# Three tiles of a chunked linear attention kernel: the transpose of r and k moved from TensorE to a DMA

## The chip, the cores and the metric

The kernel runs on one core of one Trainium2 chip. The metric is the device time of one execution in microseconds (us). Of a changed kernel, the time is told against runs of the kernel before on the same chip.

## What is computed

The reference has two parts. The first is a linear attention with a decaying state, for 4 batches and 8 heads of 768 steps and 48 features:

```
for t in range(S):
    cur = einsum('bhd,bhe->bhde', u * k[t], v[t])
    y[t] = einsum('bhd,bhde->bhe', r[t], state + cur)
    state = w[t][:, :, :, None] * state + einsum('bhd,bhe->bhde', k[t], v[t])
```

The second part takes y as 3072 rows x of 384 numbers. A gate picks the two largest of 8 logits x @ w_gate and weighs them by a softmax. The output is x plus the weighted sum of two adapters (x @ A[e]) @ B[e] of rank 16.

## The kernel before

**Tiles.** The 3072 rows are cut into 24 tiles of 128 steps, six for each batch. Within a batch a tile has index c = t % 6, and a state S passes from tile to tile; c = 0 starts afresh.

**Stages of one tile.** They are small functions, named in the plan:

- ln, csA, csB: the logarithm of w (ScalarE) and its running sum (TensorE, into the accumulator cs_ps).
- expP, expN: exp of the sum and of its negative (ScalarE, L251 and L255).
- mult (L271, the multiply at L276): r times the one and k times the other in one VectorE instruction. The result is one of four fixed buffers rk2, 128 steps x (2, 4, 2, 64) in bf16: for r and for k, four pairs of heads, each pair padded to 128 columns.
- tr (L320, L324): eight TensorE transposes of 128 x 128 blocks into the accumulator trp. trev (L328, through the helper's line L301): ScalarE copies it to the buffer rkT, of which there are three.
- amm (L333, L339): for each of the eight heads the product of transposed k and transposed r, into a_ps. aev (L343, L345): VectorE masks it into at.
- kv (L352): adds k times v into the state's accumulator. sev and szero copy it out and blank the blocks that aren't wanted.
- ymS (L373): the state's part of y, with the transposed r of rkT as weights. ymA (L383): the part within the tile.
- rkp, xk, xkev, dg, dgev, dv, ba: the term with u. xs takes y out of the accumulator.
- lg, g1, gexp, g2, g3, g4: logits and gate, for batches of one to four tiles. z, zw, zTm, zTev: adapters' inner part.
- d (L516): the outer product and, for some tiles, x itself, into an accumulator. oev (L523): the copy to one of six result buffers, by ScalarE (L295) or VectorE (L528). store (L531, L532): a DMA to the output, issued by the sync queue.

**Order.** Nothing reorders the work: the string PLAN names each step with its tile and, behind the dot, the engine that it takes. Every engine executes its own instructions in the order of the plan, and waits at each for what it needs. This holds for the sync queue too: a DMA whose data isn't there holds up those behind it. Around the change the plan runs, on that queue, load of w for tiles 22 and 23, store:7, store:8, store:4, store:9, store:6, store:10, store:13 and so on. On TensorE tr:18 stands ahead of amm:18, tr:19 behind amm:18 and ahead of amm:19, and tr:20 between amm:19 and amm:20; a mult stands ahead of its tr:

```
mult:18 ymS:17 tr:18 rkp:20 ... aev:17 ... trev:18 dg:18 d:9.2 xs:16 mult:19 amm:18 ... oev:9.2 ...
aev:18 csB:20 xk:16 tr:19 expN:20 d:8.2 kv:19 mult:20 ... trev:19 ... amm:19 sev:19 xkev:17 d:10
oev:8.2 dv:18 csB:21 kv:20 ymA:18 aev:19 oev:10 tr:20 ... trev:20 amm:20 ...
```

Above, "..." stands for steps of the plan that are left out.

Of the kernel before, what the change touches and what calls it, by code (L numbers as in the profile page):

```python
# [8 lines left out]
BF16 = mybir.dt.bfloat16  # L9
# [31 lines left out]
csB:9 g3:3 mult:8 tr:8 szero:6 xs:5 xk:5 g4:3 dgev:7 expN:9 csA:10 dv:6.1 ymA:6 ba:6.1 dv:7 zw:3 aev:7 sev:7 ymS:7  # L41
xkev:5 kv:8 expP:10 rkp:10 lg:4 zTm:3 ba:7 trev:8 rkp:9.1 xs:6.1 sev:8 ymA:7 csB:10 zTev:3.1 mult:9 xs:7 szero:8
amm:8 load_w:14 xk:6 tr:9 szero:7.1 aev:8 d:0.2 d:1 expN:10 xkev:6 trev:9 oev:0.2 rkp:11.1 mult:10 oev:1 load_v:16
kv:9 csA:11 dg:8 dg:9 amm:9 expP:11 aev:9 d:3 dgev:9 csB:11 d:2.2 xk:7 dv:8 tr:10 sev:9 oev:3 expN:11 szero:9 dv:9.1
ymS:8 xkev:7 csA:12 lg:7 store:3 trev:10 ymA:8 ba:8 dg:10 lg:5 amm:10 oev:2.2 kv:10 xs:8 mult:11 lg:6 expP:12 csB:12
ln:14 xk:8 rkp:15 expN:12 g1:7 ymS:9 xkev:8 aev:10 tr:11 rkp:12.1 mult:12 gexp:7 ba:9.1 g2:7 load_w:18 csA:13 ymA:9
lg:8 trev:11 dg:11 expP:13 dgev:11 ymS:10 amm:11 csB:13 ymA:10 load_w:16 tr:12 sev:10 xs:9.1 aev:11 dv:10 expN:13
xk:9 g3:7 csA:14 kv:12 z:7 ba:10 trev:12 mult:13 expP:14 rkp:13.1 store:0 szero:10 sev:12 g4:7 store:2 load_rk:20
xs:10 xkev:9 zw:7 csB:14 tr:13 amm:12 trev:13.1 expN:14 dv:11.1 lg:9 csA:15 dg:12 xk:10 ln:18 rkp:14 ymS:11 expP:15
zTm:7 kv:13 xkev:10 aev:12 zTev:7.1 csB:15 ba:11.1 ymA:11 d:5.2 lg:10 expN:15 dg:13 xs:11.1 amm:13 ln:16 mult:14  # L50
tr:14 mult:15 dgev:13.1 xk:11 oev:5.2 d:6 sev:13 dv:12.1 xkev:11 ymA:12 csA:16 aev:13 kv:14 lg:11 trev:14 expP:16
szero:13.1 store:1 ba:12.1 xs:12.1 sev:14.1 g1:11 oev:6 load_w:20 szero:12.1 tr:15 csB:16 dv:13 amm:14 rkp:18 xk:12
d:4 expN:16 csA:17 dg:14 kv:15 ymS:13 trev:15 aev:14 rkp:16 xkev:12 ymA:13 expP:17 dg:15 rkp:17.1 szero:14 mult:16
ba:13 ymS:14 dgev:15 ymA:14 gexp:11 oev:4 amm:15 csB:17 tr:16 xs:13 dv:14 dv:15 xk:13 expN:17 csA:18 sev:15 g2:11
xkev:13 ba:14 z:11 expP:18 kv:16 aev:15 store:5 xs:14 xk:14 csB:18 trev:16 g3:11 g4:11.1 ymS:15 ba:15 sev:16 expN:18
ymA:15 ln:20 load_w:22 mult:17 dg:16 amm:16 zw:11 xs:15 tr:17 zTm:11 xkev:14 aev:16 csA:19 lg:12 dg:17 lg:14
szero:15 trev:17 d:7.2 xk:15 szero:16 lg:13 amm:17 zTev:11.1 ymS:16 expP:19 dgev:17 oev:7.2 csB:19 store:7 rkp:19
mult:18 ymS:17 tr:18 rkp:20 ln:22 kv:18 ymA:16 dv:16 aev:17 expN:19 ba:16 xkev:15 csA:20 ymA:17 trev:18 dg:18 d:9.2
xs:16 mult:19 amm:18 dv:17.1 rkp:22.1 ba:17.1 expP:20 oev:9.2 sev:18 szero:18 xs:17.1 aev:18 csB:20 xk:16 tr:19
expN:20 d:8.2 kv:19 mult:20 csA:21 xkev:16 dg:19 xk:17 rkp:21 trev:19 dgev:19 expP:21 amm:19 sev:19 xkev:17 d:10  # L60
oev:8.2 dv:18 csB:21 kv:20 ymA:18 aev:19 oev:10 tr:20 dv:19.1 ba:18 expN:21 xs:18 lg:15 dg:20 ymS:19 csA:22 xk:18
trev:20 amm:20 rkp:23 g1:15 expP:22 z:15 csB:22 gexp:15 sev:20 g2:15 ymA:19 store:8 ba:19.1 szero:19 xkev:18 mult:21
tr:21 expN:22 store:4 lg:16 csA:23 aev:20 xs:19.1 kv:21 dg:21 store:9 trev:21 xk:19 amm:21 dgev:21 sev:21 g3:15
szero:20.1 ymS:20 mult:22 store:6 lg:17 tr:22 g4:15.1 dv:20 ymA:20 ba:20 zw:15 xkev:19 lg:19 expP:23 trev:22
store:10 aev:21 xs:20 zTm:15 lg:18 ymS:21 csB:23 dv:21.1 szero:21 ymA:21 ba:21.1 xk:20 amm:22 g1:19 zTev:15.1 d:13
expN:23 xs:21.1 dg:22 mult:23 xkev:20 gexp:19 oev:13 dg:23 g2:19 lg:20 xk:21 kv:22 d:12.2 xkev:21 aev:22 z:19 tr:23
g3:19 sev:22 d:11.2 dgev:23 g4:19 dv:22.1 lg:21 dv:23 oev:12.2 store:13 d:14 zw:19 trev:23 d:15 oev:11.2 amm:23
store:12 oev:14 g1:21 zTm:19 ymS:22 szero:22 ba:22.1 oev:15 ymA:22 zTev:19.1 d:16.2 d:17 gexp:21 xs:22.1 ymS:23
ba:23 aev:23 ymA:23 oev:16.2 xk:22 oev:17 xkev:22 clr:23 g2:21 store:11 g3:21 xs:23 z:21 lg:22 xk:23 g4:21 xkev:23
d:18 oev:18 zw:21 g1:22 zTm:21 store:14 gexp:22 lg:23 zTev:21 d:19 g1:23 d:20 z:22 g2:22 zw:22 oev:19 gexp:23 oev:20  # L70
z:23 zTm:22 store:17 zTev:22.1 g2:23 store:15 d:21.2 zw:23 zTm:23 d:22.2 store:16 store:18 oev:21.2 zTev:23.1
oev:22.2 d:23.2 oev:23.2 store:19 store:20 store:21 store:22 store:23
"""


# [16 lines left out]
def kernel(  # L92
# [9 lines left out]
    nc = tc.nc  # L102
# [7 lines left out]
    P = H // 2  # L110

    const = ctx.enter_context(tc.tile_pool(name="const", bufs=1))
    wk = ctx.enter_context(tc.tile_pool(name="wk", bufs=2))
    pp = ctx.enter_context(tc.tile_pool(name="pp", bufs=1, space=PSUM))

    st = {t: {} for t in range(-LEAD, NT)}
# [182 lines left out]
    def copy16(ch, out, in_):  # L299
        if ch == 0:  # L300
            nc.scalar.copy(out=out.bitcast(F32), in_=in_.bitcast(F32))  # L301
        else:
            nc.vector.tensor_copy(out=out, in_=in_)
# [16 lines left out]
    def tr(t, ch):  # L320
# [4 lines left out]
                                    ident)  # L325
        st[t]["trp"] = trp

    def trev(t, ch):  # L328
        x = wk.tile([128, 2, P, 128], BF16, name="rkT", bufs=3)
        copy16(ch, x, st[t]["trp"])  # L330
        st[t]["rkT"] = x
# [197 lines left out]
        st[t]["res"] = res  # L529

    def store(t, ch):  # L531
        nc.sync.dma_start(out=out[t * 128:(t + 1) * 128, :], in_=st[t]["res"])  # L532

    env = locals()
    with tc.manual_schedule(engines={ENG.PE, ENG.Activation, ENG.DVE, ENG.Pool, ENG.SP}):
# [48 lines left out]
```

## Time and profile before

| | |
|---|---|
| three timed runs | 90.38, 90.49 (median), 90.61 us |
| the profiled execution | 90.56 us |
| its span | 88.7 us |
| TensorE busy | 78.5 us |
| VectorE busy | 75.6 us |
| ScalarE busy | 72.1 us |
| GpSimd busy | 50.4 us |
| granted TensorE clock, mean | 0.994 of full speed |

In the rows of the profile PE is TensorE, DVE is VectorE, ACT is ScalarE, POOL is GpSimd and SPq the sync queue. A row of the timeline has its start and its length in us, the engine, the line of the kernel, the operation, and output <- input with the count of merged instructions. In the chain of work that ended last, a row has start, length and what was executed then. A row of the DMA issues ends with the KB of one transfer and the median time from issue to landing. A row of the table by stretches has for each engine the busy time and, in brackets, the instructions; behind them stand the granted clock, the busy share of the 16 DMA engines, and GB/s.

### The profile page before, as it was taken

The page shows a single profiled execution, that of the slowest core. Times are in us where ns is not written, and L with a number is a line of the kernel's source. Part 1 is how long each engine was busy: PE and PEld are TensorE (multiplying, and loading weights), DVE is VectorE, ACT ScalarE, POOL GpSimd, SP SyncE. Part 2 cuts the span into 40 slices and gives each one's busy share as a digit, 9 for nine tenths or more (in the row PEclk, how much of TensorE's full clock was granted, in tenths as well). Part 3 has the DMA queues.
Part 4 walks back from the last instruction along what each step waited for, and adds up shares of the span by engine and source line. Part 5 has one row for each costly group of instructions (what it writes and reads, how often), then busy time and mean ns, then how long its engine had stood idle before and what let it go on. Part 6 is the DMA issues. An engine that isn't in the chain of part 4 may idle for free.

```text
span 88.7 us, 3198 instructions
## 1 busy us (share of the span) xinstructions
PE 78.5 (89%) x1258; PEld 59.5 (67%) x1258; DVE 75.6 (85%) x181; ACT 72.1 (81%) x176; POOL 50.4 (57%) x97
## 2 busy tenths in 40 slices
PE   3898578999999999989999999999999999999600
PEld 1344446676976787668788879988778898666300
DVE  5048269999999999999999989999999899998830
ACT  2566469999999899889999997999999899776500
POOL 4980092965948497491685795698576191830000
PEclk9999999999999999999999999999999999999997
DMA  1999999999999999999999982002009200447292
GB/s 16 366 398 323 261 288 288 265 227 283 230 273 209 215 216 203 219 206 259 383 381 166 208 223 77 0 0 96 0 0 375 73 3 11 177 181 265 96 369 75
DMA packets 9103, 17.53 MB, mean 198 GB/s; under 512 B 896, under 2 KB 6016, under 8 KB 9088
## 3 DMA queue, kind: packets, MB, share of 16 engines
q0 software_dynamic: 3184, 6.69, 40.2%
q1 hardware_dynamic: 5616, 10.05, 31.2%
q10 hardware_dynamic: 288, 0.59, 1.8%
q8 instruction: 10, 0.16, 0.7%
q14 instruction: 5, 0.04, 0.1%
HBM read 19.29 MB, written 4.72 MB: 271 GB/s over the span
## 4 chain that ended last, share of the span: by engine, by line
PE 53%; ACT 14%; DVE 12%; DMA 8%; POOL 5%; issue 3%; ACTq 0%; DVEq 0%; POOLq 0%
PE trp L324 8%; DMA v<-in_v_dram 8%; PE xk_ps L407 6%; PE a_ps L339 6%; PE z_ps L483 4%; PE y_ps L383 4%; PE d_ps L520 4%; PE cs_ps L246 3%; DVE rk L276 3%; ACT rkT L301 3%; PE s_ps L352 3%; ACT e L251 3%; DVE at L345 3%; ACT logw L230 2%; PE y_ps L373 2%
## 5 line engine op out<-in xcount | busy, mean ns | idle before, releaser
L345 DVE TENSOR_TENSOR at<-a_ps,strict 128x1024 f16<-128x1024 f32 x24 | 29.0, 1206 | 0.7 <-PE a_ps L339 0.7
L314 POOL TENSOR_TENSOR dv<-v,dg 128x384 f32<-128x384 f16 (+1 forms) x23 | 20.4, 899 | 11.4 <-ACT dg L295 5.3
L324 PE MATMUL trp<-ident,rk 128*128 128x128 bf16 x192 | 14.7, 219 | 0.3 <-DVE rk L276 0.3
L301 ACT COPY rkT<-trp 128x512 f32<-128x512 f32 x22 | 13.1, 595 | 1.6 <-PE trp L324 1.5
L255 ACT ACTIVATE e<-cs_ps 128x384 bf16<-128x384 f32 x24 | 12.1, 504 | 1.8 <-PE cs_ps L246 1.4
L251 ACT ACTIVATE e<-cs_ps 128x384 bf16<-128x384 f32 x24 | 12.0, 502 | 1.7 <-PE cs_ps L242 1.7
L324 PEld LDWEIGHTS <-rk 128*128 128x128 bf16 x192 | 11.5, 97 | 2.0 <-DVE rk L276 1.0
L276 DVE TENSOR_TENSOR rk<-rk,e 128x768 bf16<-128x768 f16 x22 | 12.4, 570 | 0.2 <-ACT e L255 0.2
L368 POOL MEMSET S_sb<- 64x192 bf16 x28 | 7.1, 252 | 9.2 <-ACT S_sb L295 7.9
L301 ACT COPY xkT<-xk_ps 128x384 f32<-128x384 f32 (+1 forms) x24 | 11.0, 458 | 1.2 <-PE xk_ps L407 1.2
L339 PE MATMUL a_ps<-rkT 48*128 48x128 bf16 x192 | 9.5, 218 | 0.4 <-DVE at L345 0.2
L295 ACT CAST S_sb<-s_ps 128x384 bf16<-128x384 f32 x18 | 8.9, 496 | 0.9 <-PE s_ps L352 0.9
L230 ACT ACTIVATE logw<-w_in 128x768 f16<-128x768 f32 x11 | 9.4, 858 | 0.0
L285 DVE TENSOR_TENSOR rkp<-rk 128x384 f16<-128x384 f16 (+1 forms) x14 | 6.2, 450 | 3.5 <-DMA rk<-in_rk_dram 3.5
L383 PE MATMUL y_ps<-v,at 128*128 128x48 f16 x192 | 8.7, 183 | 0.5 <-DVE at L345 0.5
L285 POOL TENSOR_TENSOR rkp<-rk 128x384 f16<-128x384 f16 x10 | 9.0, 909 | 0.0
L383 PEld LDWEIGHTS <-at 128*128 128x128 f16 x192 | 7.3, 96 | 2.0 <-DVE at L345 0.8
L246 PE MATMUL cs_ps<-logw,ident 128*128 128x384 f16 x24 | 7.9, 330 | 0.7 <-ACT e L251 0.7
L242 PE MATMUL cs_ps<-logw,strict 128*128 128x384 f16 x24 | 8.0, 332 | 0.4 <-ACT logw L226 0.3
L407 PE MATMUL xk_ps<-ident,rkp 128*128 128x128 f16 x72 | 8.0, 219 | 0.2 <-DVE rkp L285 0.2
L339 PEld LDWEIGHTS <-rkT 48*128 48x128 bf16 x192 | 5.6, 94 | 3.7 <-ACT rkT L301 0.8
L407 PE MATMUL xk_ps<-ident,xs 128*128 128x128 f16 x72 | 7.9, 219 | 0.1
(76 smaller groups left out, 179.6 us busy)
## 6 DMA issues: line engine op xcount, KB each, us to landing
out_dram<-res SPq DMA_DIRECT2D x24, 192.0 KB, 2.3
w_in<-in_w_dram SPq DMA_DIRECT2D x11, 384.0 KB, 7.0
rk<-in_rk_dram POOLq DMA_DIRECT2D x3, 768.0 KB, 17.6
rk<-in_rk_dram POOLq DMA_DIRECT2D x5, 384.0 KB, 12.7
v<-in_v_dram POOLq DMA_DIRECT2D x5, 384.0 KB, 15.3
rk<-in_rk_dram SPq DMA_DIRECT2D x1, 384.0 KB, 4.5
rk<-in_rk_dram ACTq DMA_DIRECT2D x1, 384.0 KB, 4.8
v<-in_v_dram POOLq DMA_DIRECT2D x2, 192.0 KB, 8.5
```

What stands on the lines that cost most here:

```text
L230: nc.scalar.activation(out=x, in_=st[t]["w"], func=ACT.Ln)
L251: nc.scalar.activation(out=e2[:, 0], in_=cs_ps[:, 0:HD], func=ACT.Exp)
L255: nc.scalar.activation(out=st[t]["e2"][:, 1], in_=cs_ps[:, 0:HD], func=ACT.Exp, scale=-1.0)
L276: nc.vector.tensor_mul(rk2s[t % 4].rearrange("s m p h d -> s (m p h) d")[:, :, 0:D], st[t]["rk"].rearrange("s m (h d) -> s (m h) d", d=D), ...
L285: (nc.gpsimd, nc.vector)[ch].tensor_mul(x, st[t]["r"], st[t]["k"])
L301: nc.scalar.copy(out=out.bitcast(F32), in_=in_.bitcast(F32))
L314: (nc.gpsimd, nc.gpsimd, nc.vector)[ch].tensor_mul(x, st[t]["v16"], st[t]["dg"].rearrange("p (h o) -> p h o", o=1).to_broadcast([L, H, D]))
L324: nc.tensor.transpose(trp[:, m, p, :], st[t]["rk2"][:, m, p, :, :].rearrange("s a b -> s (a b)"), ident)
L339: nc.tensor.matmul(a_ps[:, g, p, :], lhsT=rkT[base:base + D, 1, p, :], rhs=rkT[base:base + D, 0, p, :], start=True, stop=True)
L345: nc.vector.tensor_mul(at, st[t]["a_ps"].rearrange("s g p f -> s (g p) f"), strict.to_broadcast([128, H, 128]))
L383: nc.tensor.matmul(y_ps[:, h, :], lhsT=st[t]["at"][:, g * P + p, :], rhs=st[t]["v16"][:, h, :], start=(c == 0 and h == 0), stop=(h == H - ...
L407: nc.tensor.transpose(xk_ps[:, 3 * q + j, :], src[:, j * 128:(j + 1) * 128], ident16)
```

## The change

A new step trd takes the place of tr and trev for tiles 18, 19 and 20. It issues one DMA on the sync queue that reads the scaled r and k (128 x 1024 in bf16) from rk2 and writes them, transposed block by block, into rkT. It stands in the plan where tr stood. The words of the stores are moved in the plan to stand soon behind their oev; the order of the sync queue's stores among each other and against the loads is as before, and the three DMAs stand behind store:7 (tiles 18 and 19, one after the other) and behind store:10 (tile 20). All other instructions of every engine keep their order. The store can now name another queue, which no word of the plan does.

```
 around the change, in PLAN:
-mult:18 ymS:17 tr:18 rkp:20 ln:22 kv:18 ymA:16 dv:16 aev:17 expN:19 ba:16 xkev:15 csA:20 ymA:17 trev:18 dg:18 d:9.2
-xs:16 mult:19 amm:18 dv:17.1 rkp:22.1 ba:17.1 expP:20 oev:9.2 sev:18 szero:18 xs:17.1 aev:18 csB:20 xk:16 tr:19
-expN:20 d:8.2 kv:19 mult:20 csA:21 xkev:16 dg:19 xk:17 rkp:21 trev:19 dgev:19 expP:21 amm:19 sev:19 xkev:17 d:10
-oev:8.2 dv:18 csB:21 kv:20 ymA:18 aev:19 oev:10 tr:20 dv:19.1 ba:18 expN:21 xs:18 lg:15 dg:20 ymS:19 csA:22 xk:18
-trev:20 amm:20 rkp:23 g1:15 expP:22 z:15 csB:22 gexp:15 sev:20 g2:15 ymA:19 store:8 ba:19.1 szero:19 xkev:18 mult:21
-tr:21 expN:22 store:4 lg:16 csA:23 aev:20 xs:19.1 kv:21 dg:21 store:9 trev:21 xk:19 amm:21 dgev:21 sev:21 g3:15
-szero:20.1 ymS:20 mult:22 store:6 lg:17 tr:22 g4:15.1 dv:20 ymA:20 ba:20 zw:15 xkev:19 lg:19 expP:23 trev:22
-store:10 aev:21 xs:20 zTm:15 lg:18 ymS:21 csB:23 dv:21.1 szero:21 ymA:21 ba:21.1 xk:20 amm:22 g1:19 zTev:15.1 d:13
+store:7 csB:19 rkp:19 mult:18 ymS:17 trd:18 rkp:20 ln:22 kv:18 ymA:16 dv:16 aev:17 expN:19 ba:16 xkev:15 csA:20
+ymA:17  dg:18 d:9.2 xs:16 mult:19 amm:18 dv:17.1 rkp:22.1 ba:17.1 expP:20 oev:9.2 sev:18 szero:18 xs:17.1
+aev:18 csB:20 xk:16 trd:19 expN:20 d:8.2 kv:19 mult:20 csA:21 xkev:16 dg:19 xk:17 rkp:21  dgev:19 expP:21
+amm:19 sev:19 xkev:17 d:10 oev:8.2 store:8 store:4 store:9 store:6 dv:18 csB:21 kv:20 ymA:18 aev:19 oev:10 store:10
+trd:20 dv:19.1 ba:18 expN:21 xs:18 lg:15 dg:20 ymS:19 csA:22 xk:18  amm:20 rkp:23 g1:15 expP:22 z:15 csB:22
...
+    def trd(t, ch):
+        x = wk.tile([128, 2, P, 128], BF16, name="rkT", bufs=3)
+        nc.sync.dma_start(out=x.rearrange("p m q f -> p (m q) f"),
+                          in_=st[t]["rk2"].rearrange("s m p h d -> s (m p h d)"), transpose=True)
+        st[t]["rkT"] = x
...
     def store(t, ch):
-        nc.sync.dma_start(out=out[t * 128:(t + 1) * 128, :], in_=st[t]["res"])
+        (nc.sync, nc.scalar)[ch].dma_start(out=out[t * 128:(t + 1) * 128, :], in_=st[t]["res"])
```

More of the change, by code (lines that the diff above doesn't have):

```diff
@@ L43 @@
 amm:8 load_w:14 xk:6 tr:9 szero:7.1 aev:8 d:0.2 d:1 expN:10 xkev:6 trev:9 oev:0.2 rkp:11.1 mult:10 oev:1 load_v:16
[L44 to L57, printed above, removed]
@@ L63 @@
-tr:21 expN:22 store:4 lg:16 csA:23 aev:20 xs:19.1 kv:21 dg:21 store:9 trev:21 xk:19 amm:21 dgev:21 sev:21 g3:15
-szero:20.1 ymS:20 mult:22 store:6 lg:17 tr:22 g4:15.1 dv:20 ymA:20 ba:20 zw:15 xkev:19 lg:19 expP:23 trev:22
-store:10 aev:21 xs:20 zTm:15 lg:18 ymS:21 csB:23 dv:21.1 szero:21 ymA:21 ba:21.1 xk:20 amm:22 g1:19 zTev:15.1 d:13
-expN:23 xs:21.1 dg:22 mult:23 xkev:20 gexp:19 oev:13 dg:23 g2:19 lg:20 xk:21 kv:22 d:12.2 xkev:21 aev:22 z:19 tr:23
-g3:19 sev:22 d:11.2 dgev:23 g4:19 dv:22.1 lg:21 dv:23 oev:12.2 store:13 d:14 zw:19 trev:23 d:15 oev:11.2 amm:23
@@ L68 @@
[L68 to L72, printed above, removed]
+kv:9 csA:11 dg:8 dg:9 amm:9 expP:11 aev:9 d:3 dgev:9 csB:11 d:2.2 xk:7 dv:8 tr:10 sev:9 oev:3 store:3 expN:11
@@ new lines @@
+szero:9 dv:9.1 ymS:8 xkev:7 csA:12 lg:7 trev:10 ymA:8 ba:8 dg:10 lg:5 amm:10 oev:2.2 kv:10 xs:8 mult:11 lg:6 expP:12
+csB:12 ln:14 xk:8 rkp:15 expN:12 g1:7 ymS:9 xkev:8 aev:10 tr:11 rkp:12.1 mult:12 gexp:7 ba:9.1 g2:7 load_w:18 csA:13
+ymA:9 lg:8 trev:11 dg:11 expP:13 dgev:11 ymS:10 amm:11 csB:13 ymA:10 load_w:16 store:0 store:2 store:1 tr:12 sev:10
+xs:9.1 aev:11 dv:10 expN:13 xk:9 g3:7 csA:14 kv:12 z:7 ba:10 trev:12 mult:13 expP:14 rkp:13.1 szero:10 sev:12 g4:7
+load_rk:20 xs:10 xkev:9 zw:7 csB:14 tr:13 amm:12 trev:13.1 expN:14 dv:11.1 lg:9 csA:15 dg:12 xk:10 ln:18 rkp:14
@@ new lines @@
+ymS:11 expP:15 zTm:7 kv:13 xkev:10 aev:12 zTev:7.1 csB:15 ba:11.1 ymA:11 d:5.2 lg:10 expN:15 dg:13 xs:11.1 amm:13
+ln:16 mult:14 tr:14 mult:15 dgev:13.1 xk:11 oev:5.2 d:6 sev:13 dv:12.1 xkev:11 ymA:12 csA:16 aev:13 kv:14 lg:11
+trev:14 expP:16 szero:13.1 ba:12.1 xs:12.1 sev:14.1 g1:11 oev:6 load_w:20 store:5 szero:12.1 tr:15 csB:16 dv:13
+amm:14 rkp:18 xk:12 d:4 expN:16 csA:17 dg:14 kv:15 ymS:13 trev:15 aev:14 rkp:16 xkev:12 ymA:13 expP:17 dg:15
+rkp:17.1 szero:14 mult:16 ba:13 ymS:14 dgev:15 ymA:14 gexp:11 oev:4 amm:15 csB:17 tr:16 xs:13 dv:14 dv:15 xk:13
@@ new lines @@
+expN:17 csA:18 sev:15 g2:11 xkev:13 ba:14 z:11 expP:18 kv:16 aev:15 xs:14 xk:14 csB:18 trev:16 g3:11 g4:11.1 ymS:15
+ba:15 sev:16 expN:18 ymA:15 ln:20 load_w:22 mult:17 dg:16 amm:16 zw:11 xs:15 tr:17 zTm:11 xkev:14 aev:16 csA:19
+lg:12 dg:17 lg:14 szero:15 trev:17 d:7.2 xk:15 szero:16 lg:13 amm:17 zTev:11.1 ymS:16 expP:19 dgev:17 oev:7.2
+store:7 csB:19 rkp:19 mult:18 ymS:17 trd:18 rkp:20 ln:22 kv:18 ymA:16 dv:16 aev:17 expN:19 ba:16 xkev:15 csA:20
+ymA:17  dg:18 d:9.2 xs:16 mult:19 amm:18 dv:17.1 rkp:22.1 ba:17.1 expP:20 oev:9.2 sev:18 szero:18 xs:17.1
@@ new lines @@
+aev:18 csB:20 xk:16 trd:19 expN:20 d:8.2 kv:19 mult:20 csA:21 xkev:16 dg:19 xk:17 rkp:21  dgev:19 expP:21
+amm:19 sev:19 xkev:17 d:10 oev:8.2 store:8 store:4 store:9 store:6 dv:18 csB:21 kv:20 ymA:18 aev:19 oev:10 store:10
+trd:20 dv:19.1 ba:18 expN:21 xs:18 lg:15 dg:20 ymS:19 csA:22 xk:18  amm:20 rkp:23 g1:15 expP:22 z:15 csB:22
+gexp:15 sev:20 g2:15 ymA:19 ba:19.1 szero:19 xkev:18 mult:21 tr:21 expN:22 lg:16 csA:23 aev:20 xs:19.1 kv:21 dg:21
+trev:21 xk:19 amm:21 dgev:21 sev:21 g3:15 szero:20.1 ymS:20 mult:22 lg:17 tr:22 g4:15.1 dv:20 ymA:20 ba:20 zw:15
@@ new lines @@
+xkev:19 lg:19 expP:23 trev:22 aev:21 xs:20 zTm:15 lg:18 ymS:21 csB:23 dv:21.1 szero:21 ymA:21 ba:21.1 xk:20 amm:22
+g1:19 zTev:15.1 d:13 expN:23 xs:21.1 dg:22 mult:23 xkev:20 gexp:19 oev:13 store:13 dg:23 g2:19 lg:20 xk:21 kv:22
+d:12.2 xkev:21 aev:22 z:19 tr:23 g3:19 sev:22 d:11.2 dgev:23 g4:19 dv:22.1 lg:21 dv:23 oev:12.2 store:12 d:14 zw:19
+trev:23 d:15 oev:11.2 store:11 amm:23 oev:14 store:14 g1:21 zTm:19 ymS:22 szero:22 ba:22.1 oev:15 ymA:22 zTev:19.1
+d:16.2 d:17 gexp:21 xs:22.1 ymS:23 ba:23 aev:23 ymA:23 oev:16.2 xk:22 oev:17 store:17 store:15 store:16 xkev:22
@@ L73 @@
+clr:23 g2:21 g3:21 xs:23 z:21 lg:22 xk:23 g4:21 xkev:23 d:18 oev:18 store:18 zw:21 g1:22 zTm:21 gexp:22 lg:23
+zTev:21 d:19 g1:23 d:20 z:22 g2:22 zw:22 oev:19 store:19 gexp:23 oev:20 store:20 z:23 zTm:22 zTev:22.1 g2:23 d:21.2
+zw:23 zTm:23 d:22.2 oev:21.2 store:21 zTev:23.1 oev:22.2 store:22 d:23.2 oev:23.2 store:23
 """
```

## The prediction

> **What bounds the kernel now.** I read the page first, for the length and the chain that ended last.
>
> ```profile
> span 88.7 us, 3198 instructions
> ...
> PE 53%; ACT 14%; DVE 12%; DMA 8%; POOL 5%; issue 3%; ACTq 0%; DVEq 0%; POOLq 0%
> ```
>
> The profiled execution took 90.56 us, so 1.9 us lie outside its span; the median of the three runs shown is 90.49, and a sum made against 90.56 stands for it within 0.1 us. Over half of the chain is TensorE, so I went to the chain in order of time around the three tiles.
>
> ```profile
> 60.94 0.47 PE trp L324 x8
> ...
> 63.63 0.45 PE trp L324 x8
> ...
> 66.44 0.45 PE trp L324 x8
> ...
> 75.83 0.45 PE trp L324 x8
> ```
>
> There are 24 groups of eight transposes, in the order of the tiles, and the last of them, at 75.83, is tile 23's; two more (69.51 and 71.60 in the same view) lie between it and 66.44. So the first three rows are tiles 18, 19 and 20, and what the change takes from TensorE stands on the chain: 0.47 + 0.45 + 0.45 = 1.37 us.
>
> What the chain does not show is how close a transposed tile is to its reader. For that I read the timeline from 60 to 68 us.
>
> ```profile
> 60.17 0.55 DVE L276 TENSOR_TENSOR rk<-rk,e 128x768 bf16<-128x768 f16 x1
> ...
> 62.35 0.55 DVE L276 TENSOR_TENSOR rk<-rk,e 128x768 bf16<-128x768 f16 x1
> ...
> 62.47 0.40 PE L339 MATMUL a_ps<-rkT 48*128 48x128 bf16 x8
> ...
> 63.55 1.22 DVE L345 TENSOR_TENSOR at<-a_ps,strict 128x1024 f16<-128x1024 f32 x1
> ...
> 64.69 0.55 DVE L276 TENSOR_TENSOR rk<-rk,e 128x768 bf16<-128x768 f16 x1
> ...
> 65.08 0.40 PE L339 MATMUL a_ps<-rkT 48*128 48x128 bf16 x8
> 65.15 0.54 DVE L528 TENSOR_TENSOR res<-xs,d_ps 128x384 f32<-128x384 f16 x1
> ...
> 66.01 0.53 ACT L295 COPY res<-d_ps 128x384 f32<-128x384 f32 x1
> ...
> 67.80 0.40 PE L339 MATMUL a_ps<-rkT 48*128 48x128 bf16 x8
> ```
>
> The L276 rows are mult:18, 19 and 20, which make the scaled r and k; the L339 rows are amm:18, 19 and 20, the first readers of the transposed tile; L345 is aev:18; L528 is oev:8 and L295 oev:10. From the end of the multiply to the reader there are 62.47 - 60.72 = 1.75 us for tile 18, 65.08 - 62.90 = 2.18 for tile 19 and 67.80 - 65.24 = 2.56 for tile 20. TensorE meets its instructions in order, so a tile that isn't there stops everything behind its amm.
>
> **The change part by part.**
>
> *Removed from TensorE and ScalarE.* With 0.45 us of transposes gone, TensorE reaches amm:18 at about 62.0 and could, if nothing were late, gain 1.37 us in all. The three ScalarE copies are replaced by the landing of the DMA in the same place, so I give them no price of their own: what counts is when the tile is there.
>
> *Added: three DMAs, price unknown.* No row shows a transposing DMA. Its tile is 128 x 1024 bf16, 256 KB. Call L its time from issue to landing. The nearest rows are the other transfers that the chip makes without GpSimd:
>
> ```profile
> out_dram<-res SPq DMA_DIRECT2D x24, 192.0 KB, 2.3
> w_in<-in_w_dram SPq DMA_DIRECT2D x11, 384.0 KB, 7.0
> ...
> rk<-in_rk_dram SPq DMA_DIRECT2D x1, 384.0 KB, 4.5
> ...
> w<-in_w_dram SPq DMA_DIRECT2D x1, 192.0 KB, 3.1
> ```
>
> The lower end is the store, 2.3 us: the same kind of queue, fewer bytes, whole rows. The upper end is the w load in the crowded middle of the kernel, 7.0. A negative end is excluded, since a tile cannot land before it is issued. Between the two loads that the sync queue issued at the start, 192 KB in 3.1 us and 384 KB in 4.5, 256 KB falls at 3.1 + 1.4 x 64 / 192 = 3.6 us. I take 3.6, my estimate, as the row nearest in size, the 3.1, carries fewer bytes and the larger load more.
>
> The Trainium skill can be read both ways here. Its page Advanced Engine Details and Errata (X-Bar Transpose) says that transposing DMAs are as fast as ordinary ones, and gives 350 to 400 GB/s; with the fixed 2.0 us of DMA: Bandwidth & Descriptors (Anatomy of one DMA) an estimate from these pages is 2.7 us, and the sum below would give 93.4 us. No run here shows a transpose as yet.
>
> *Tile 18.* Ahead of it on the sync queue stands one store:
>
> ```profile
> 60.28 0.33 SPq L532 DMA_DIRECT2D out_dram<-res  x1
> ```
>
> It is through at 60.61, before mult:18 ends at 60.72. So the DMA is issued at about 60.75 and lands at 60.75 + L = 64.35. amm:18 starts there and not at 62.47: 1.9 us late, with TensorE idle for 64.35 - 62.0 = 2.3 us.
>
> *Tile 19.* mult:19 needs nothing behind amm:18 and still ends at 62.90; its DMA is issued at once and lands at 66.5. TensorE needs 65.08 - 62.47 - 0.45 = 2.16 us from amm:18 to amm:19 and comes there at 66.51. Nothing more is lost; amm:19 is 1.4 us late.
>
> *Tile 20, where most is lost.* Its DMA is late twice. First, its tile is: aev:18 follows amm:18 on VectorE, mult:20 follows aev:18, and oev:8 follows mult:20. Second, it stands behind five stores on the sync queue (store:8, 4, 9, 6 and 10), and the first of them waits for oev:8. In the trace of before these five are:
>
> ```profile
> 65.72 2.32 SPq L532 DMA_DIRECT2D out_dram<-res  x5
> ```
>
> So after oev:8 ends (65.69 before) the queue is free 68.04 - 65.69 = 2.35 us later, already later than the 67.80 at which amm:20 runs today. That holds however fast the transpose is. In the changed kernel: amm:18 ends at 64.75, aev:18 takes 1.22, mult:20 ends 65.24 - 64.77 = 0.47 after it, and oev:8 another 65.69 - 65.24 = 0.45 after that: 66.89. Plus 2.35 is 69.24, where the third DMA is issued. store:10 itself needs oev:10, which ends 66.54 - 65.08 = 1.46 after amm:19 starts, at 67.97, in time for its place among the five. The tile lands at 69.24 + 3.6 = 72.84, and amm:20 is 72.84 - 67.80 = **5.04 us late**. TensorE has come there at 66.51 + (67.80 - 65.08 - 0.45) = 68.78 and is idle for 4.1 us.
>
> In general the shift at amm:20 is 2L - 2.16, since L is paid at tile 18 and again at tile 20. Below L = 2.4 aev:18 is held by its engine and not by amm:18, and the third DMA leaves at 68.04: the shift is then L + 0.24, or 2.54 for 2.3.
>
> *Behind it.* The moved words of the plan change nothing more on the sync queue: its 24 stores and its loads keep their order, and the DMAs only come between store:7 and store:8 and behind store:10. What is left of the kernel is shifted whole, but for idle time that the shift can fill:
>
> ```profile
> 67.80:77.20 9.40, 9.40 (x174) 7.71 (x172) 9.06 (x27) 8.20 (x23) 4.53 (x11) 1.00 0.25 90
> 77.20:84.50 7.30, 6.45 (x79) 3.91 (x78) 6.47 (x26) 4.66 (x15) 1.35 (x5) 1.00 0.51 185
> ```
>
> The columns are the stretch, its length, and the busy time of TensorE, its weight loads, VectorE, ScalarE and GpSimd. Up to 77.2 TensorE is busy throughout; behind that it has 7.30 - 6.45 = 0.85 us free. I let half of it, 0.4 us, be won back.
>
> *Sum.* 90.56 + 5.04 - 0.4 = **95.2 us**; the 1.37 us of TensorE are inside the 5.04, spent in waiting.
>
> **The rivals.**
>
> *The clock falls as well.* The end of the trace shows what the clock does when TensorE is idle:
>
> ```profile
> 87.00:88.00 1.00, 0.00 (x0) 0.00 (x0) 0.00 (x0) 0.00 (x0) 0.00 (x0) 0.86 0.00 0
> 88.00:88.70 0.70, 0.00 (x0) 0.00 (x0) 0.00 (x0) 0.00 (x0) 0.00 (x0) 0.50 0.00 0
> ```
>
> The last column but two is the granted clock: 0.50 at the end, and a mean of 0.86 in the last full microsecond, so it fell at 88.00 - 0.28 = 87.72. The chain has its last matmul here:
>
> ```profile
> 84.18 0.35 PE d_ps L520
> ```
>
> That is 3.2 us of idleness, and tile 20's wait is 4.1. If the clock falls there and needs as long to return, TensorE does 3.2 us at half speed and loses 1.6: 96.8 us. Against it: the idle 2.3 us at tile 18 are too short, and before the end of the kernel TensorE had been half idle already. The Trainium skill, TensorE: Matmul & The Clock Gate (Part 1), puts both windows at about 3.4 us and lets them run free of the kernel, so that 4.1 us may or may not hold a whole one; the drop above agrees with it.
>
> *A quick landing.* At 2.3 us, the store's, the shift is 2.54: 92.7 us; at 3.0 it is 3.84: 94.0. For it: the tile never leaves the chip, as a store's bytes do. Against it: it is a third larger than the store.
>
> *A slow transpose.* At 4.5 us the shift is 6.84: 97.0 us. At 7.0, 11.84: 102.0 us. For it: tile 20's DMA follows five stores on one queue, and where six stores of before came close together (60 to 70 us) they took 4.1 us to land instead of 2.3:
>
> ```profile
> out_dram<-res SPq DMA_DIRECT2D x6, 192.0 KB, 4.1
> ```
>
> Against it: for tiles 18 and 19 the queue is nearly empty. The Trainium skill, VectorE: DVE Perf Modes (The three transpose paths), has 1309 ns for one 128 x 128 block by DMA against 390 by TensorE; eight in turn would be an estimate of 10.5 us, and 109 us for the kernel.
>
> *Not slower.* With L at 2.3 the delay of 2.54 us could be absorbed behind amm:20. It would take all idleness that the two rows above can hold: 0.85 in the second, and 9.40 - 7.71 = 1.69 in the first if time without a weight load is taken as free. That gives 90.56, and it decides only from L = 2.3 down. Against it: TensorE's matmuls fill those 9.40 us.
>
> **How the numbers follow.** Forecast, L from 3 to 4.5 with the full clock: 0.42. Clock falls as well: 0.18. Quick landing, L under 3: 0.20. Slow transpose, L over 4.5: 0.17. Not slower: 0.03. The range runs from 92.5, just under the store's landing, to 102.0, the slow load's. This kernel's measurement tells about 0.3% from no change; faster has 0.01, same 0.02, slower 0.97.
>
> **What would show it.** amm:18 waiting on a DMA for about 2.3 us; amm:19 with little or no wait; amm:20 waiting about 4 us, its DMA issued right behind store:10; the granted clock under 1 behind that wait, or not. The step on tile 20 is wrong if its wait is no longer than tile 18's. The forecast is wrong if a transposing DMA lands in less than 2.3 us or more than 7, or if issuing it holds the sync queue so long that tile 19 waits too.

## The result and the profile after

The changed kernel takes 98.86 us (median of 4 runs, 98.41 to 99.60) against 90.44 us before: **1.094 times as long**, 95% interval 1.090 to 1.098. The profiled execution took 99.60 us with a span of 97.9 us, 9.2 us more than the 88.7 of before. Some executions of several kernels, the one before included, take over 1.5% longer than the fastest, mostly at a lower granted clock; the times and ratios below leave these out.

The page of the changed kernel, in the order of reading of before: the span, the busy shares and the granted clock over 40 slices, the chain that ended last.

```profile
span 97.9 us, 3155 instructions
...
PE   4785589999999998999999999659903999999720
...
PEclk9999999999999999999999999995885579999997
...
PE 51%; DMA 16%; ACT 13%; DVE 10%; issue 3%; POOL 2%; ACTq 0%; DVEq 0%
DMA rkT<-rk 8%; DMA v<-in_v_dram 7%; PE trp L324 7%; PE a_ps L345 6%; PE xk_ps L413 6%; PE y_ps L389 4%; PE cs_ps L246 4%; PE z_ps L489 4%; PE d_ps L526 3%; PE s_ps L358 3%; ACT rkT L301 3%; DVE at L351 3%; PE cs_ps L242 2%; DVE rk L276 2%; PE cs_ps L237 2%
```

DMAs have doubled their share of the chain, 8% to 16%, and the new 8% are the transposes. TensorE has two dips (659 and 903), and the clock two dips that begin a little later than TensorE's and last longer. Both are new; the same two rows of before are:

```profile
PE   3898578999999999989999999999999999999600
...
PEclk9999999999999999999999999999999999999997
```

The chain in order of time through the three tiles (start, length, what ran; L345 is now amm, L330 the transposing DMA):

```profile
61.30 3.48 DMA rkT<-rk
64.83 0.40 PE a_ps L345 x8
...
67.97 0.54 PE a_ps L345 x8
...
70.24 4.71 DMA rkT<-rk
75.00 0.61 PE a_ps L345 x8
```

The first DMA is tile 18's, the second tile 20's; tile 19's is nowhere on the chain. amm:18, 19 and 20 stand at 64.83, 67.97 and 75.00. In the same view of before they stood here, so they are 2.3, 2.8 and 7.1 us late:

```profile
62.54 0.33 PE a_ps L339 x8
...
65.15 0.33 PE a_ps L339 x8
...
67.87 0.33 PE a_ps L339 x8
```

The queue that issued the DMAs:

```profile
60.70 0.33 SPq L538 DMA_DIRECT2D out_dram<-res  x1
61.30 3.30 SPq L330 DMA_TRANSPOSE rkT<-rk  x2
67.49 2.66 SPq L538 DMA_DIRECT2D out_dram<-res  x5
70.24 1.24 SPq L330 DMA_TRANSPOSE rkT<-rk  x1
```

That is the order that the prediction drew: one store, two transposes, five stores, the third transpose right behind. mult:20 ended at 67.0 (66.44 + 0.56 in the timeline), 3.2 us ahead of its DMA. The row of the five stores holds a wait: the last of them, store:10, was issued at 69.81, right behind its oev:10, which ended at 69.79 (69.31 + 0.48 in the timeline). The tile's own view gives the three landings:

```profile
DMA to landing us min/median/max: 3.1/3.5/4.7
```

Last, the stretches of 2 us (length, busy TensorE, weight loads, VectorE, ScalarE, GpSimd; then the granted clock):

```profile
64.00:66.00 2.00, 1.17 (x17) 0.87 (x18) 0.73 (x1) 0.47 (x2) 0.89 (x2) 0.98 0.80 151
66.00:68.00 2.00, 2.00 (x20) 1.35 (x20) 1.46 (x3) 1.42 (x6) 0.40 (x1) 0.50 0.00 0
68.00:70.00 2.00, 2.00 (x32) 1.31 (x33) 1.22 (x1) 1.37 (x4) 2.00 (x3) 0.66 0.86 323
70.00:72.00 2.00, 1.05 (x14) 0.63 (x10) 1.61 (x8) 1.43 (x5) 0.59 (x3) 1.00 0.75 226
72.00:74.00 2.00, 0.00 (x0) 0.00 (x0) 0.00 (x0) 0.16 (x1) 0.33 (x2) 0.69 1.45 79
74.00:76.00 2.00, 1.00 (x13) 0.81 (x14) 0.35 (x1) 0.00 (x0) 0.00 (x0) 0.50 0.02 3
76.00:78.00 2.00, 2.00 (x23) 1.66 (x21) 1.54 (x6) 0.50 (x2) 0.00 (x0) 0.50 0.00 0
78.00:80.00 2.00, 2.00 (x26) 1.66 (x24) 1.24 (x3) 1.18 (x4) 0.00 (x0) 0.60 0.00 0
80.00:82.00 2.00, 2.00 (x50) 1.79 (x48) 1.43 (x2) 1.85 (x6) 1.75 (x3) 1.00 0.00 0
```

Between 66 and 68 us TensorE is "busy" throughout and does 20 matmuls; between 80 and 82 it does 50. These are of different sizes, but the same eight of amm took 0.40 us at 64.83 and 0.61 at 75.00 in the chain above. With only 1.00 and 0.50 as levels (no stretch shows less than 0.50), the edges follow from the means: 0.98 over 2 us is 0.08 us at half speed, so the clock fell at 65.92; 0.66 is 1.36 us, back at 69.36; 0.69 is 1.24 us, down at 72.76; 0.60 is 1.6 us, back at 79.60. TensorE worked at half speed for 3.4 us behind the first wait and for 4.6 us (75.00 to 79.60) behind the second.

### The profile page after: what moved, and what is told of

It reads as the page before. It is cut to its first block, busy times and chain, and to the rows that moved or that the text cites. A ratio compares the mean times of both kernels' runs of the same rounds, so it can differ in the third digit from the quotient of the medians.

```text
span 97.9 us, 3155 instructions
## 1 busy us (share of the span) xinstructions
PE 80.9 (83%) x1234; PEld 60.4 (62%) x1234; DVE 76.2 (78%) x181; ACT 71.2 (73%) x173; POOL 50.6 (52%) x97
## 3 DMA queue, kind: packets, MB, share of 16 engines
q1 hardware_dynamic: 8784, 10.84, 34.3%
## 4 chain that ended last, share of the span: by engine, by line
PE 51%; DMA 16%; ACT 13%; DVE 10%; issue 3%; POOL 2%; ACTq 0%; DVEq 0%
DMA rkT<-rk 8%; DMA v<-in_v_dram 7%; PE trp L324 7%; PE a_ps L345 6%; PE xk_ps L413 6%; PE y_ps L389 4%; PE cs_ps L246 4%; PE z_ps L489 4%; PE d_ps L526 3%; PE s_ps L358 3%; ACT rkT L301 3%; DVE at L351 3%; PE cs_ps L242 2%; DVE rk L276 2%; PE cs_ps L237 2%
## 5 line engine op out<-in xcount | busy, mean ns | idle before, releaser
L345 PE MATMUL a_ps<-rkT 48*128 48x128 bf16 x192 | 10.0, 225 | 6.2 <-DMA rkT<-rk 5.8
L324 PE MATMUL trp<-ident,rk 128*128 128x128 bf16 x168 | 13.3, 224 | 0.3 <-DVE rk L276 0.3
L301 ACT COPY rkT<-trp 128x512 f32<-128x512 f32 x19 | 11.3, 595 | 1.5 <-PE trp L324 1.3
L345 PEld LDWEIGHTS <-rkT 48*128 48x128 bf16 x192 | 5.9, 97 | 9.7 <-DMA rkT<-rk 6.2
L324 PEld LDWEIGHTS <-rk 128*128 128x128 bf16 x168 | 10.5, 100 | 2.1 <-DVE rk L276 1.0
L526 PE MATMUL d_ps<-Ball,zT 128*128 128x384 f16 x24 | 8.1, 338 | 0.1
```

The source lines that it names most:

```text
L324: nc.tensor.transpose(trp[:, m, p, :], st[t]["rk2"][:, m, p, :, :].rearrange("s a b -> s (a b)"), ident)
L345: nc.tensor.matmul(a_ps[:, g, p, :], lhsT=rkT[base:base + D, 1, p, :], rhs=rkT[base:base + D, 0, p, :], start=True, stop=True)
```

## The experiments

My theory after this: the loss is TensorE waiting for the landing, paid at tile 18 and again at tile 20, where five stores are ahead in the queue; and each wait costs a second time through the clock. The rivals: the transposing DMAs slow other work by themselves; the stores have no part in it; the clock costs nothing because something else is the bound then. All ratios are against runs of the kernel before on the same chip, with 95% intervals.

### One tile at a time, and the DMA of tile 20 ahead of the stores

The first three kernels each keep one trd and put back tr and trev for the other two tiles; here for tile 18:

```
-... csB:20 xk:16 trd:19 expN:20 ... rkp:21 dgev:19 ... store:10 trd:20 dv:19.1 ...
+... csB:20 xk:16 tr:19 expN:20 ... rkp:21 trev:19 dgev:19 ... store:10 tr:20 dv:19.1 ... trev:20 amm:20 ...
```

The fourth keeps all three and moves one word:

```
-... d:8.2 kv:19 mult:20 csA:21 ... oev:8.2 store:8 store:4 store:9 store:6 ... oev:10 store:10 trd:20 ...
+... d:8.2 kv:19 mult:20 trd:20 csA:21 ... oev:8.2 store:8 store:4 store:9 store:6 ... oev:10 store:10 ...
```

> Only tile 18 is transposed by the DMA; tiles 19 and 20 by TensorE and ScalarE again. If the loss is the landing on the path plus a clock that falls behind the wait: amm:18 waits about 2 us, the clock goes to 0.5 behind it for some 3.4 us as in the changed kernel, and the kernel takes 93.5 us (between 92.5 and 94.5). If the clock costs nothing, 92.2 us. If the DMA only hurts by taking queue or memory from other work, under 91 us.

> Only tile 19 is transposed by the DMA. By the first theory its landing (about 3.1 to 3.5 us behind the end of mult:19) is some 1.6 us behind the time at which TensorE gets there without its transposes, too short a wait for the clock to fall: 91.5 us (91.0 to 92.0), clock 1.00 throughout. If every such wait drops the clock, about 93 us. If tile 19 costs nothing, as its missing wait in the changed kernel may suggest, 90.0 to 90.4.

> Only tile 20 is transposed by the DMA, behind the five stores. If the queue of stores is the cause, the DMA is issued at about 68 us though mult:20 ends at 65.2, lands some 4.7 us later, amm:20 is about 5 us late and the clock falls in the wait: 97 us (96 to 98), more than half of the whole loss and more than tile 18 alone. If the landing alone is the cause and not the stores, about the same as tile 18 alone, 93.5.

> As the changed kernel, but the DMA of tile 20 stands right behind mult:20 in the plan and so ahead of the five stores. If the stores ahead of it are the cause of tile 20's wait: the DMA is issued at about 67 us and lands at 70.3, before TensorE gets to amm:20; the 3.95 us wait and the slow clock behind it go: 92.8 us (92.0 to 94.0), about the same as tile 18 alone. If tile 20 waits for another reason (contention, a long landing of the transpose itself), 97 us or more.

| kernel | time, us | ratio to before | landing, us | wait at amm, us |
|---|---|---|---|---|
| tile 18 alone | 92.81 | 1.027 (1.014 to 1.040) | 3.2 | 1.6 |
| tile 19 alone | 91.43 | 1.012 (1.005 to 1.020) | 3.1 | 1.2 |
| tile 20 alone | 97.91 | 1.087 (1.078 to 1.096) | 3.5 | 5.2 |
| all three, tile 20 ahead of the stores | 93.04 | 1.027 (1.021 to 1.032) | 3.1 | 1.5, at tile 18 only |

Tile 18's time stands on two runs, 92.12 and 93.50 us. The trace is of the second; the first is what was expected if the clock costs nothing. Whether the clock fell behind the wait there too isn't known.

Tile 20 alone costs 7.5 of the 8.4 us. Its queue tells why, from its trace:

```profile
60.44 9.06 SPq L538 DMA_DIRECT2D out_dram<-res  x6
69.61 1.33 SPq L330 DMA_TRANSPOSE rkT<-rk  x1
```

The multiply of tile 20 ended at 65.39 us there, and its DMA was issued 4.2 us later, behind the last of the six stores; the landing itself took 3.5 us, against 3.1 to 3.2 in the other three. One of these stores held the queue for 1.78 us, where its neighbours took 0.33 to 0.45. One word moved ahead of the stores takes 5.8 us off the changed kernel (98.86 to 93.04) and leaves it at tile 18's price. So the stores are the larger part of the cause, shown from both sides. The three single losses (2.4, 1.0 and 7.5 us) add up to more than the changed kernel's 8.4: a tile's wait gives the next tile time.

The granted clock in the run with tile 18 alone (same columns as above):

```profile
62.00:64.00 2.00, 0.49 (x12) 0.24 (x10) 1.48 (x4) 0.88 (x2) 1.11 (x4) 1.00 0.69 131
64.00:66.00 2.00, 1.88 (x17) 1.35 (x18) 1.22 (x1) 0.80 (x2) 0.43 (x1) 0.51 0.00 0
66.00:68.00 2.00, 2.00 (x24) 1.70 (x22) 1.11 (x2) 1.13 (x3) 0.00 (x0) 0.64 0.00 0
```

A wait of 1.6 us was enough: down at 64.04, back at 67.44. With tile 19 alone and its wait of 1.2 us the clock stayed at 1.00 from 16 us up to the last stores. It was not 1.00 throughout, though that was expected: between 10 and 16 us, long before the change, the stretches of 2 us show 0.95, 0.50 and 0.70, so it was down from 11.8 to 15.2. In that execution (92.12 us) mult:18 began 1.0 us later than before (61.19 instead of 60.17), and amm:19 ran 2.2 us later (67.25 instead of 65.08), so that 1.2 of these are tile 19's own. The fastest run with tile 19 alone took 90.95 us, 0.5 us more than the kernel before.

### The same DMAs with nobody waiting

TensorE and ScalarE transpose as before; three DMAs at the changed kernel's places write a buffer that isn't read.

```
+    def trx(t, ch):
+        x = wk.tile([128, 2, P, 128], BF16, name="rkX", bufs=3)
+        nc.sync.dma_start(out=x..., in_=st[t]["rk2"]..., transpose=True)
 in PLAN, for t = 18, 19, 20:   -trd:t   +tr:t trx:t ... trev:t
```

> Tiles 18, 19 and 20 are transposed by TensorE and ScalarE as before; the same three DMAs are issued besides, at the changed kernel's places, into a buffer that nobody reads. If the loss is waiting for the landing, the DMAs themselves cost nothing: 90.4 us (90.1 to 90.9), clock full. If the transposing DMAs slow other work (memory, queue, clock), a good part of the 8.4 us stays: over 92 us.

Measured: 90.63 us, ratio 1.0035 (1.001 to 1.006). So 0.3 of the 8.4 us can be laid to the transfers themselves, and the rest to waiting for them. TensorE had no wait for a transposed tile and a full clock from 44 to 84 us.

### The waits filled with idle work

```
-... xs:16 mult:19 amm:18 ...          xk:18 amm:20 ...
+... xs:16 mult:19 warm:18.11 amm:18 ... xk:18 warm:20.22 amm:20 ...
```

warm issues matmuls of ones into the accumulator that the product then overwrites.

> As the changed kernel, with matmuls of 128 x 384 that nobody reads in TensorE's two waits: 11 ahead of amm:18 (1.8 us) and 22 ahead of amm:20 (3.6 us), into the accumulator that the product then overwrites. If the slow clock behind the waits is a part of the loss of its own, the granted clock stays 1.00 and the kernel takes 95.6 us (94.8 to 96.4), near the forecast without the clock. If the clock costs nothing, 98.9 us or a little more.

Measured: 96.72 us, ratio 1.071 (1.065 to 1.078), against 98.86 for the changed kernel. The clock was 1.00 in every stretch from 60 to 80 us, so 2.1 us of the loss were the clock's, and 6.3 us the waits'. By the two intervals the 2.1 us are uncertain by 0.7. The clock's part may also be a little more than that, since the idle work ahead of amm:18 ended at 64.37 us, 0.3 us behind the landing (60.94 + 3.13 = 64.07), and so cost something itself. The 2.1 us are less than the 3.3 us that I expected from it, and the time is just above the expected range. Its chain is the prediction's sum without the clock: the third DMA issued at 69.50, right behind store:10, landed in 4.2 us, and

```profile
62.42 1.95 PE L173 MATMUL a_ps<-ones 128*128 128x384 f16 x11
64.43 0.40 PE L345 MATMUL a_ps<-rkT 48*128 48x128 bf16 x8
66.95 0.40 PE L345 MATMUL a_ps<-rkT 48*128 48x128 bf16 x8
69.50 3.74 PE L173 MATMUL a_ps<-ones 128*128 128x384 f16 x22
73.70 0.40 PE L345 MATMUL a_ps<-rkT 48*128 48x128 bf16 x8 [0.46 <-DMA rkT<-rk]
```

amm:20 at 73.70 is 5.9 us behind the 67.80 of before, and its span (94.6) 5.9 us longer than 88.7: the delay at amm:20 went to the end whole.

### Half the bytes

Tile 18 only, k by DMA and r by four transposes and a half copy.

```
+    def trh(t, ch):
+        x = wk.tile([128, 2, P, 128], BF16, name="rkT", bufs=3)
+        nc.sync.dma_start(out=x[:, 1], in_=st[t]["rk2"][:, 1]..., transpose=True)
+        ...                       # trp[:, 0, p, :] from rk2[:, 0, p] by TensorE, as in tr
+    def trhev(t, ch):
+        copy16(ch, st[t]["rkT"][:, 0], st[t]["trp"][:, 0])
 in PLAN:   -trd:18   +trh:18 ... trhev:18
```

> Only tile 18, and of it only k by DMA (half the bytes); r by four transposes on TensorE and a ScalarE copy of half a tile. It measures how the landing grows with size: with the whole tile it was 3.2 us of which 1.4 in the issue. If the landing is mostly fixed, 2.4 to 2.7 us, and a wait of about 0.9 us at amm:18; if it goes with the bytes, 1.6 us and no wait. The kernel: 91.0 us (90.4 to 92.0), the clock full if the wait is short enough.

Measured: 91.87 us, ratio 1.015 (1.011 to 1.018), landing 2.6 us, wait 1.0 us, clock full. Half the bytes land only 0.6 us sooner than the whole tile's 3.2, so on these two points about 2.0 us are fixed. If that line holds for smaller ones, of which none was run, no transpose by DMA would fit in the 1.75 us that tile 18 has.

### With the landing hidden

Here the running sum, the exps and the multiply (and the logarithm of tiles 16 and 17) are moved earlier in the plan, by a share of a tile that grows to a whole tile at tile 18 and stays so; each DMA stands right behind its mult. The control has the same lead with TensorE's transposes.

```
 tiles 13 to 23, csA expP csB expN mult: place in the plan moved towards that of the tile before
 in the DMA kernel, for t = 18, 19, 20:   -tr:t ... trev:t   mult:t +trd:t
```

> No DMA transpose at all: the kernel before with the running sum, the two exps and the multiply of tiles 13 to 23 moved earlier in the plan, by a share of a tile that grows to one whole tile from tile 18 on. A control for the next run. It removes no work: 90.4 us, between 89.5 and 91.5.

> The same lead, and tiles 18, 19 and 20 by DMA, each issued right behind its multiply and ahead of the five stores. With one tile more of lead, some 4.4 us from multiply to reader, a landing of 3.1 to 3.5 us is hidden. If waiting is the whole cost, no wait for rkT stays, the clock is full, and the kernel is faster than its control by up to the 1.37 us of TensorE's transposes: 89.2 us (88.8 to 90.2). If the DMA costs something besides, it is slower than its control.

Measured: the control 92.94 us, 1.031 (1.026 to 1.036); with the DMAs 92.56 us, 1.026 (1.024 to 1.028). The lead itself costs 2.5 us, which I hadn't expected, and the 89.2 us expected with the DMAs were missed by 3.4. With the lead TensorE's list of waits has no DMA of rkT any more, and the clock is full up to 88 us. The landing at tile 18 is only just hidden: it took 4.7 us there and ended at 65.04, and amm:18 ran at 65.09, the control's 65.10. The DMAs are ahead of their control by 0.4 us, with intervals that overlap; not by 1.37. From amm:17, which no DMA feeds, to amm:23 the control takes 79.66 - 62.49 = 17.17 us and the kernel with the DMAs 79.53 - 62.40 = 17.13; the kernel before took 77.23 - 59.93 = 17.30. So the lead's loss is there before the first DMA counts, and behind it the pace is the old one. The two in the stretch of the three tiles, control first:

```profile
60.00:64.00 4.00, 4.00 (x86) 3.49 (x83) 4.00 (x7) 4.00 (x11) 3.36 (x5) 1.00 0.08 24
64.00:68.00 4.00, 4.00 (x73) 2.93 (x70) 4.00 (x8) 3.76 (x11) 2.51 (x6) 1.00 0.08 29
```

```profile
60.00:64.00 4.00, 3.87 (x82) 3.27 (x79) 4.00 (x7) 4.00 (x10) 3.43 (x6) 1.00 0.57 88
64.00:68.00 4.00, 3.85 (x55) 2.31 (x55) 4.00 (x8) 3.09 (x9) 2.52 (x5) 1.00 0.78 162
```

TensorE and ScalarE get free time there; VectorE (third of the five) is full in both. I took VectorE for the bound, and tested that together with a shorter run-up of the lead:

```
 lead grows over tiles 16 to 18 instead of 13 to 18
 in the two last kernels:   -d:9.2 oev:9.2 d:8.2 oev:8.2   +d:9 oev:9 d:8 oev:8
```

> As the kernel with the lead and the three DMAs, but the lead grows within three tiles (16 to 18) and not six, so the logarithm of tiles 16 and 17 isn't moved ahead of its place; the earlier lead left VectorE idle for some 1.5 us of 44 to 54 us. No wait for rkT and a full clock in both theories. If the lead's own cost was mainly that place: 91.0 us (90.2 to 92.0). If it was the whole squeeze: 92.5 us again.

> As e9_late_lead, and the outputs of tiles 8 and 9 are copied by ScalarE instead of VectorE, which takes some 1.1 us off VectorE and gives 1.0 us to ScalarE and 0.33 us to TensorE in the stretch around the three tiles. If VectorE bounds that stretch once the waits are gone (it was busy 4.00 of 4.00 us there with the lead, with and without the DMAs), this is 0.5 to 1.1 us faster than e9_late_lead. If TensorE bounds it, 0.3 us slower.

> As e10_results_act, with TensorE's transposes and ScalarE's copies for tiles 18, 19 and 20 instead of the DMAs: the control for what the DMA is worth when VectorE has room. If TensorE and ScalarE are the next bound, it is 0.7 to 1.4 us slower than e10_results_act. If the DMA is worth nothing even then, within 0.4 us of it.

| kernel | time, us | ratio to before |
|---|---|---|
| shorter run-up, DMAs | 92.53 | 1.022 (1.019 to 1.026) |
| the same, two outputs copied by ScalarE | 93.11 | 1.029 (1.025 to 1.032) |
| the last, without the DMAs | 93.27 | 1.032 (1.029 to 1.035) |

The place of the run-up doesn't matter: amm:17 ran at 62.40 us with the longer one and at 62.41 with the shorter, 2.5 us later than before. That leaves the squeeze of a tile's work into an already full stretch as the cost; that is argued and not shown. In the kernel with the shorter run-up the landing was not hidden: tile 18's DMA took 4.9 us and stands on the chain. With 1.1 us less of VectorE's work the kernel was 0.6 us slower and not faster, and taking TensorE's and ScalarE's transposes away from that one saves 0.2 us. The chains that ended last tell more; here are the shares of the engines with the lead and the DMAs, with the shorter run-up, with the copies on ScalarE, and the last without the DMAs:

```profile
DVE 36%; PE 28%; ACT 12%; issue 8%; DMA 7%; POOL 5%; DVEq 0%; POOLq 0%
...
PE 28%; ACT 24%; DVE 20%; DMA 13%; issue 6%; POOL 5%; DVEq 0%; ACTq 0%; POOLq 0%
...
ACT 31%; PE 29%; DVE 17%; DMA 7%; issue 6%; POOL 5%; DVEq 0%; ACTq 0%; POOLq 0%
...
PE 42%; ACT 20%; DVE 18%; DMA 7%; POOL 5%; issue 4%; DVEq 0%; ACTq 0%; POOLq 0%
```

With the lead VectorE has the largest share (its control shows 36% too), where the kernel before had 53% on TensorE and 12% on VectorE. With the shorter run-up tile 18's landing is in it, and no engine stands out. With the copies on ScalarE, ScalarE leads; with the transposes back, TensorE. So the longest chain goes where work is moved to, and in this stretch no engine has room to take any: that is read from one execution of each. No kernel of these is faster than the one before.

## Why the prediction was right, and where it was off

*What bounds, and the slack between multiply and reader.* Right. The measured waits stand at amm:18 and amm:20 and not at amm:19, as drawn.

*The landing, L = 3.6 us.* Right in size: 3.0 to 3.6 us for most of the transposes of a whole tile, and 4.2 to 4.7 for tile 20 behind the stores in the changed kernel and in the one with filled waits. But the stores are not the whole reason: with the unused DMAs tile 20's landed in 3.0 us behind the same five, and with the lead tile 18's took 4.7 to 4.9 with no store just ahead. Why is open. The prediction's estimate of 2.7 us from the Trainium skill was too short for every whole tile; the 2.0 us in it (DMA: Bandwidth & Descriptors, Anatomy of one DMA) are given there for DMAs that GpSimd issues. The rule of the Trainium skill that transposes are as fast as ordinary DMAs (Advanced Engine Details and Errata, X-Bar Transpose) agrees better than its 1309 ns a block (VectorE: DVE Perf Modes, The three transpose paths): eight blocks in 3.1 us are under 400 ns a block, landing included.

*Tile 18, 1.9 us late, TensorE idle for 2.3.* The trace has a wait of 1.9 us and a start 2.3 us later, of which 0.4 was there already when mult:18 began (60.59 instead of 60.17). Right on the start. The idle time was less than 2.3 us because TensorE came to its wait no sooner than before: the second half of ymA:17, a few steps ahead, starts only when aev:17 is done (at 62.33, behind 61.05 + 1.22; before at 61.94, behind 60.64 + 1.21). So the 0.45 us of transposes were not free to be gained there.

*Tile 19, no wait.* Right, but amm:19 came 2.8 us late instead of 1.4. From amm:18 to amm:19 TensorE took 67.97 - 64.83 = 3.1 us, not 2.16: the slow clock.

*Tile 20, behind the stores.* Right in mechanism, and shown by the kernel that moves the one word. Its DMA was issued at 70.24 instead of 69.24 and took 4.7 us instead of 3.6, so amm:20 was 7.1 us late instead of 5.0. One premise failed: oev:10 was to end at 67.97, "in time for its place among the five". It ended at 69.79, behind a d:10 at half the clock, and store:10 and the third DMA waited for it. With the filled waits and a full clock the DMA was issued at 69.50.

*The step that failed* is the clock: "the idle 2.3 us at tile 18 are too short". It fell behind both waits, and I had given it 0.18 and 1.6 us for tile 20 alone. I took the 3.2 us at the kernel's end for the idle time that is needed; 1.6 us were enough. The filled waits put its price at 2.1 us or a little more of the 3.7 between 95.2 and 98.86. The rest is the longer landing at tile 20 (0.6 us by the same run), its later issue (0.3), and the 0.4 us that I let be won back: with the clock full, nothing was. These make 3.4 us; the 0.3 that remain are less than the uncertainty of the 2.1.

*Luck.* The case that I held most likely, a full clock and a landing of 3 to 4.5 us, is not what came. Two rivals came at once, the falling clock and, at tile 20, a landing over 4.5 us. 98.86 us lies in the range because that reached to 102.0 for a slow landing, not because the sum had the falling clock at both tiles.

*The gain behind the loss.* I counted TensorE's 1.37 us as a gain that the waits ate. With the waits hidden, 0.4 us or less of it could be seen, where VectorE had the largest share of the chain and the DMAs take no work off VectorE. That didn't touch the forecast, but it would have misled a better placed version.

## What to carry to other kernels

Before a hand-over between engines is replaced by a DMA, set the landing (here 2.6 us for 128 KB, 3.0 to 4.9 us for 256 KB) against the time from the last write to the first read in the reader's own order, and add what stands ahead of it in the issuing queue with the waits of those DMAs: that queue cost more here than the landing. A wait of TensorE can be paid again at half the clock for some 3.4 us or twice that, so price it from 1.5 us up. And work taken off an engine that is busy all the time is worth only what the other full engines let through; test that first with the latency hidden.

## What the runs showed of the hardware

- The clock's edges lie on a grid: 65.92, 69.36, 72.76 and 79.60 us are 3.44, 3.40 and 2 x 3.42 us apart, and with tile 18 alone 64.04 and 67.44 are 3.40 apart. This agrees with the window of 3413 ns in the Trainium skill, TensorE: Matmul & The Clock Gate (Part 1). That page speaks of an idle window; here the window from 62.5 to 65.92 had TensorE at work again from 64.83, and the clock fell all the same, 1.1 us after the wait was over.
- In the window ahead of each fall TensorE was busy for about half of 3.41 us or less: 1.53 (62.52 to 65.93) and 1.70 (69.35 to 72.76) in the changed kernel, 1.76 (60.62 to 64.03) with tile 18 alone, 1.62 (8.39 to 11.80) with tile 19 alone. In the two windows that hold tile 19's wait of 1.2 us it was busy for 3.01 and 2.59 us, and the clock stayed. The limit isn't sharp: with tile 20 alone the window from 8.70 to 12.11 held 1.73 us, and the clock stayed. The prediction's row at the kernel's end fits this: the 3.2 us of idleness there are less than one whole window.
- Issuing a transpose holds the sync queue for 1.23 us or more, a store for 0.33 at least.
- Three transposes raise the packets of the sync queue's DMAs from 5616 to 8784, 1056 each, and those under 512 bytes by the same number.
- The issue of five stores took 2.3 us before and 3.6 us with the unused DMAs, though nothing that they waited for was later. With tile 20 alone by DMA it was 3.6 us too, with no transpose ahead of them. In both, one store of the five took 1.8 us instead of 0.45. Why is open.
